# Token high parts from the uncorrected reciprocal root, first transform loads from a second queue, a written order for groups 1 to 7

## The chip, the cores and the metric

The kernel runs on one core of one Trainium2 chip. The metric is the device time of one execution in microseconds (us); lower is better. A time is given as the median of several executions; the profile is of one further execution, with every instruction's start and length. Engines are named as in the profile: PE is TensorE's matmul and PEld its weight load, DVE is VectorE, ACT is ScalarE, POOL is GpSimd, SP is SyncE, which here only issues DMAs.

## What is computed

```python
xn = (x - mean) / sqrt(var + 1e-5)            # x: 2048 tokens x 640
a, b = xn @ dft_hid_re.T, xn @ dft_hid_im.T   # 640 x 640
y = dft_seq_re @ a - dft_seq_im @ b           # 2048 x 2048
h = relu(xn @ W_gate) * (xn @ W_up)           # 640 x 1728
out = x + y + h @ W_down
```

All in float32. The change touches the layernorm `xn` and the first products of the sequence transform with it.

## The kernel before

**Split operands.** Each float32 operand of a matmul is split into a high part (rounded to the matmul's type) and a low part (the rest). A product is three matmuls, high x high, high x low and low x high (`mm3`, lines 129 to 131; `wh`, `wl` are the parts of the weight, `mh`, `ml` those of the moving operand). ScalarE makes a high part by a copy, VectorE the low part by a subtraction (`split`, lines 123 and 124).

**Stages.** First the sequence transform is applied to the normalised tokens, then come gate and up, then the projection. Only the beginning of the first stage is touched. The 2048 tokens form 8 groups (`NG`) of 256: two tiles (`SG`) of 128 partitions each. Groups 0 to 3 have their split tokens in `xs_early`, 4 to 7 in `xs_late`. The transform's output positions form four chunks `c` of 512. The first streams are `B11` (groups 0 to 3) and `B21` (groups 4 to 7), and they run in the order group 0 chunk 0, group 0 chunk 1, group 1 chunk 0, and so on to group 7. Each such pair of group and chunk loads 512 KB of the transform matrix into `raw` (six buffers), splits it into a ring buffer `cb` (three buffers) and runs 18 matmuls into three PSUM banks, two of key `e1` and one of key `v1`. At group 3 the banks' sums are copied out by ScalarE into `sa` (chunk 0) and `sb` (chunk 1); groups 4 to 7 go on adding into the same banks.

**Layernorm of a group.** `ln_load` (198) brings the tokens. `ln_stats` (203, 204) takes two half statistics and an aggregate per tile on VectorE. `ln_root` takes the root (210) on ScalarE, its reciprocal (213) on VectorE, and corrects it by one Newton step of three small VectorE instructions (215 to 217), for which ScalarE prepares the variance with epsilon (211) and the negated mean (212). The corrected `r` stands in `stat`. Then the tokens are centred and scaled, split into high and low parts, and the last 256 columns are kept apart by a DMA from GpSimd (`keep_a21`, 234).

**The order.** Instructions of each engine run in the order in which they are recorded; a scheduler chooses this order from due times, except where `tc.keep_in_program_order` pins an instruction at its place, or `tc.issue_after` holds it behind another. `first_group` pins group 0 by hand, tile by tile. Its token high part waits for the corrected `r` (`ln_scale`, 229 and 230). The first product (`first_products`, 493) has its own order of matmuls, and GpSimd helps with three of the low parts (289). `second_group` handles group 1 with part of its work pinned (products: `second_products`, 465). `layernorm` handles groups 2 to 7, nothing of which is pinned: it scales both tiles in place (246 on VectorE, 247 on ScalarE), copies the high part (120) and subtracts for the low part (251). From group 2 on all products are `product` with `mm3`: one bank after another, 6 matmuls each.

`drive` walks the list `todo` of (load, prepare, run, finish): loads four steps ahead, preparation two steps ahead of the matmuls, and `finish` (the copies out of the banks) one step behind them. All loads are issued by SyncE, in the order x tile 0, chunk 0 half 0, chunk 1 half 0, x tile 1, chunk 1 half 1, chunk 0 half 1, and then tokens and transform blocks in turn.

Of the kernel before, what the change touches and what calls it, by code (L numbers as in the profile page):

```python
# [7 lines left out]
F32 = mybir.dt.float32  # L8
# [4 lines left out]
P = 128  # L13
# [45 lines left out]
def fnet_reglu_kernel(  # L59
# [40 lines left out]
    wparts = dram_p.tile([P, NPAIR, NW], F32, name="wparts")  # L100
    nc.vector.memset(eps_t, EPS)

    root_t = keep.tile([P, 1], F32, name="root_t")
    nc.scalar.activation(root_t, eps_t, AF.Sqrt)

# [85 lines left out]
    def ln_tiles(g):  # L191
        return (ln_place(g),
                small.tile([P, SG, 2, nc.vector.BN_STATS_DIM], F32, name="bs"),
                small.tile([P, SG, 7], F32, name="mv"))

# [10 lines left out]
    def ln_root(g, mv, js, between=()):  # L206
# [19 lines left out]
    def ln_scale(g, xs, j, cs):  # L226
        xc, r = xs[:, j, cs], stat[:, 1, g, j : j + 1]
        h, l = (tokens(g)[:, j * XS + o : j * XS + o + D][:, cs] for o in (0, D))
        yield nc.scalar.activation(h, xc, AF.Copy, scale=r)
        yield nc.vector.scalar_tensor_tensor(l, xc, r, h.bitcast(F32), op0=OP.mult, op1=OP.subtract)  # L230
# [4 lines left out]

    def layernorm(g):
        xs, bs, mv = ln_tiles(g)
        js = slice(0, SG)

        with tc.issue_after(late["ln"]):  # L240
            for i in ln_stats(g, xs, bs, mv, js):
                pass
            for i in ln_root(g, mv, js):
                late["ln"] = i.ins
            nc.vector.tensor_tensor(mv[:, 1, 6:7], stat[:, 0, g, 1:2], stat[:, 1, g, 1:2], op=OP.mult)
            late["norm"] = nc.vector.tensor_scalar(xs[:, 0], xs[:, 0], mv[:, 0, 0:1], stat[:, 1, g, 0:1], op0=OP.subtract, op1=OP.mult).ins
            nc.scalar.activation(xs[:, 1], xs[:, 1], AF.Identity, bias=mv[:, 1, 6:7], scale=stat[:, 1, g, 1:2])
            cs = K14 if g < NH else slice(0, D)
            src = xs[:, :, cs]
            high = copy(xn_block(g, cs, 0), src)  # L250
            low = nc.vector.tensor_tensor(xn_block(g, cs, 1), src, xn_block(g, cs, 0).bitcast(F32), op=OP.subtract)
            if g < NH:
                keep_a21(g)
        if g == 2:
            with tc.issue_after(high.ins), tc.issue_after(low.ins):
                st = stage()[:, :CH].rearrange("p (j d) -> p j d", j=SG)
                for j in range(SG):
                    nc.scalar.activation(st[:, j], ln_place(0)[:, j, K2], AF.Copy, scale=stat[:, 1, 0, j : j + 1])
                keep_a21(0, st)
# [3 lines left out]
    def second_group():  # L263

        xs, bs, mv = late["second"]
        js = slice(0, SG)
        nm, r = (stat[:, i, 1, js] for i in range(2))
        with tc.issue_after(late["ln"]):
            for i in ln_root(1, mv, js):
                tc.keep_in_program_order(i)  # L270
            nmr = mv[:, js, 6]
            late["ln"] = tc.keep_in_program_order(nc.vector.tensor_tensor(nmr, nm, r, op=OP.mult)).ins
            highs = [nc.scalar.activation(xn_block(1, K14, 0)[:, j], xs[:, j, K14], AF.Identity,
                                          bias=mv[:, j, 6:7], scale=stat[:, 1, 1, j : j + 1]) for j in range(SG)]
            for j in range(SG):
                nc.vector.tensor_scalar(xs[:, j], xs[:, j], mv[:, j, 0:1], stat[:, 1, 1, j : j + 1],
                                        op0=OP.subtract, op1=OP.mult)
            low = nc.vector.tensor_tensor(xn_block(1, K14, 1), xs[:, :, K14], xn_block(1, K14, 0).bitcast(F32), op=OP.subtract)
            keep_a21(1)
        late["first"] = [i.ins for i in highs + [low]]  # L280

    def first_group(b):
# [11 lines left out]
        j0, j1 = slice(0, 1), slice(1, 2)  # L294
        d0, d14, rest, every = slice(0, P), slice(P, 3 * P), slice(P, D), slice(0, D)
# [9 lines left out]
        pin(ln_center(0, xs, mv, 0, rest, nc.vector))  # L305
        pin(some(h14, 1))
        pin(high(1, 0))
        pin(h0)
        pin(h14)
        pin(behind(0, token_low(0)))  # L310
        pin(low(nc.gpsimd, 0, 0))
        pin(high(0, 1))
        pin(ln_stats(0, xs, bs, mv, j1))
        pin(low(nc.vector, 1, 0))
        pin(ln_root(0, mv, j1))
        pin(behind(1, stat[:, 1, 0, 1:2]))
        pin(low(nc.gpsimd, 0, 1))
        pin(some(second, 4))
        pin(ln_center(0, xs, mv, 1, every, nc.scalar))
        h0, h14 = ln_scale(0, xs, 1, d0), ln_scale(0, xs, 1, d14)  # L320
        pin(some(h0, 1))
        pin(some(h14, 1))
        pin(high(1, 1))
        pin(h0)
        pin(h14)
        pin(behind(1, token_low(1)))
        pin(low(nc.gpsimd, 1, 1))
        late["ln"] = pin(second)[-1].ins

# [127 lines left out]

    def second_products(b):

        keys = [("e1", 0), ("e1", 1), "v1"]  # L460
        for js, vs in (((0,), (0, 2)), ((1,), (0, 2)), ((0, 1), (1,))):
            for j in js:
                for v in vs:
                    for d, key in zip((0, 1, 4), keys):
                        nc.tensor.matmul(E[0, key], xn_part(SG + j, d)[v == 1], b[:, int(v == 2), j], start=False, stop=False)  # L465

# [17 lines left out]
    def first_products(j, b):  # L484

        keys = [("e1", 0), ("e1", 1), "v1"]
        for v, cs in (((0, (0,)), (1, (0,)), (0, (1,)), (1, (1,)), (2, (0,)), (2, (1,))),
                      ((0, (0,)), (0, (1,)), (2, (0,)), (1, (0,)), (1, (1,)), (2, (1,))))[j]:
            for c in cs:
                for d, key in zip((0, 1, 4), keys):  # L490
                    if j == 0 and v == 0:
                        E[c, key] = bank()
                    nc.tensor.matmul(E[c, key], xn_part(j, d)[v == 1], b[c][0][:, int(v == 2), j],  # L493
                                     start=j == 0 and v == 0, stop=False)
# [18 lines left out]

    start = {}

    def first_stream(c, name, g):
# [5 lines left out]
        norm = {0: 0 if n == 0 else None, 1: n + 1 if n < NG - 1 else None}.get(c)  # L522

        def load():
            if n == 0 and c == 0:
                st = start["raw"] = [raw(), raw()]
                for j in range(SG):
                    ln_load(0, slice(j, j + 1))
                    for k in range(2):
                        i = (k + j) % 2  # L530
                        nc.sync.dma_start(st[i][:, j * CH : (j + 1) * CH], dft[i, 0, 0][:, j * CH : (j + 1) * CH])
                return
            if norm is not None:
                tc.keep_in_program_order(ln_load(norm, slice(0, SG)))
            if n > 0 or c > 1:
                t["s"] = raw()
                nc.sync.dma_start(t["s"], dft[c, 0, n])

        def prepare():
            if norm == 0:  # L540
                start["b"] = [(parts(), st) for st in start["raw"]]
                first_group(start["b"])
                return
            if norm is not None:
                (second_group if norm == 1 else lambda: layernorm(norm))()
            if n > 0 or c > 1:
                t["b"] = b = parts()

                with ExitStack() as order:
                    for i in {(0, 1): [late["ln"]], (1, 1): late.get("first"), (0, 2): [late.get("norm")]}.get((c, n), ()):  # L550
                        order.enter_context(tc.issue_after(i))
                    split(flat(b, 0), flat(b, 1), t["s"])
# [17 lines left out]

        todo.append((load, prepare, run, finish))

# [684 lines left out]
```

## Time and profile before

| | us |
|---|---|
| three timed executions | 1034.75, 1036.84, 1037.27 |
| median | 1036.84 |
| the profiled execution's own time | 1032.92 |
| its span, first to last instruction | 1031.2 |
| TensorE busy in the span | 1022.8 |

How to read the profile: a row of the timeline has the start, the length, the engine, the source line, the operation, what it writes and reads (tile names without their numbers), the shapes, the count of instructions merged into the row, and in brackets how long the engine was idle before it and what released it. A row of the grouped view has a count, the busy time in us, the mean length in ns, and the idle time ahead with its releasers. A row of waits has the engine, tile and line that waited, for whom, the sum in us, how often, and the longest. Matmuls overlap: their length is about 0.39 us, but in a full stream one starts every 0.227 us.

### The profile page before, as it was taken

How to read it: one execution, taken by the hardware profiler on the slowest of the kernel's cores; microseconds unless marked ns; L12 is line 12 of the kernel's file. 1: busy time of each engine (PE TensorE's matmuls, PEld its weight loads, DVE VectorE, ACT ScalarE, POOL GpSimd, SP SyncE). 2: the span in 40 equal slices, each digit the busy share in tenths (PEclk: the TensorE clock that was granted, in tenths of full speed). 3: DMA queues.
4: the chain of work that ended last, by engine and by line, in shares of the span. 5: the costliest groups of instructions: out<-in, count | busy, mean ns of one | idle time of the engine just before them, and what ended most of it. 6: DMA issues, size and time to landing. Idle time of an engine off the chain costs nothing.

```text
span 1031.2 us, 12409 instructions
## 1 busy us (share of the span) xinstructions
PE 1022.8 (99%) x4528; PEld 844.3 (82%) x4528; DVE 800.9 (78%) x1072; ACT 433.3 (42%) x543; POOL 96.6 (9%) x161
## 2 busy tenths in 40 slices
PE   8999999999999999999999999999999999999998
PEld 7888888888888888888888888888888888888886
DVE  7947986978979897688878988886597667886764
ACT  6754443333333543333335443443355423552531
POOL 2000010101211001321110000000000000000000
PEclk9999999999999999999999999999999999999999
DMA  7975744957968864863364665654599647986543
GB/s 301 370 241 163 259 157 143 312 209 254 326 195 298 314 206 153 273 227 133 142 250 143 225 235 215 226 224 156 178 350 296 193 129 225 373 304 222 156 153 122
DMA packets 100156, 233.29 MB, mean 226 GB/s; under 512 B 11392, under 2 KB 50816, under 8 KB 98688
## 3 DMA queue, kind: packets, MB, share of 16 engines
q1 hardware_dynamic: 83088, 163.82, 47.4%
q0 software_dynamic: 17008, 68.69, 18.4%
q8 instruction: 35, 0.57, 0.2%
q14 instruction: 25, 0.20, 0.1%
HBM read 177.41 MB, written 54.02 MB: 224 GB/s over the span
## 4 chain that ended last, share of the span: by engine, by line
PE 96%; DVE 2%; issue 1%; DMA 1%; POOL 0%; SPq 0%; ACT 0%; POOLq 0%; DVEq 0%; ACTq 0%
PE ps L131 31%; PE ps L130 31%; PE ps L129 31%; PE ps L1154 1%; DMA rw<-hd 1%; DVE cb L124 0%; PE ps L493 0%; PE ps L465 0%; POOL cb L289 0%; DVE tk L605 0%; DVE raw L605 0%; DVE st L385 0%; DVE st L378 0%; SPq L1161 0%; DVE st L379 0%
## 5 line engine op out<-in xcount | busy, mean ns | idle before, releaser
L131 PE MATMUL ps<-cb,wt 128*128 128x512 f32 x390 | 151.9, 390 | 0.4 <-DVE wt L124 0.4
L129 PE MATMUL ps<-cb,wt 128*128 128x512 f32 x390 | 151.9, 390 | 0.0
L130 PE MATMUL ps<-cb,wt 128*128 128x512 f32 x390 | 151.8, 389 | 0.0
L124 DVE TENSOR_TENSOR cb<-rw,cb 128x1024 fp32r<-128x1024 f32 x83 | 94.0, 1133 | 68.6 <-ACT cb L123 67.9
L123 ACT ACTIVATE cb<-rw 128x1024 fp32r<-128x1024 f32 x83 | 82.0, 987 | 147.9 <-PE ps L131 127.2
L123 ACT ACTIVATE cb<-raw 128x1024 fp32r<-128x1024 f32 x78 | 82.5, 1059 | 123.5 <-PE ps L131 101.8
L124 DVE TENSOR_TENSOR cb<-raw,cb 128x1024 fp32r<-128x1024 f32 x78 | 95.2, 1221 | 38.9 <-ACT cb L123 38.6
L131 PE MATMUL ps<-xs_early,gw 128*128 128x512 f32 x260 | 101.2, 389 | 0.0
L130 PE MATMUL ps<-xs_early,gw 128*128 128x512 f32 x260 | 101.2, 389 | 0.0
L129 PE MATMUL ps<-xs_early,gw 128*128 128x512 f32 x260 | 101.1, 389 | 0.0
L130 PE MATMUL ps<-cb,xs_late 128*128 128x512 f32 x256 | 99.7, 390 | 0.1
L131 PE MATMUL ps<-cb,xs_late 128*128 128x512 f32 x256 | 99.6, 389 | 0.0
L129 PE MATMUL ps<-cb,xs_late 128*128 128x512 f32 x256 | 99.4, 389 | 0.0
L130 PE MATMUL ps<-cb,xs_early 128*128 128x512 f32 x238 | 92.7, 389 | 0.0
L131 PE MATMUL ps<-cb,xs_early 128*128 128x512 f32 x238 | 92.4, 389 | 0.0
L129 PE MATMUL ps<-cb,xs_early 128*128 128x512 f32 x238 | 92.2, 390 | 0.0
L120 ACT ACTIVATE gw<-z 128x1024 fp32r<-128x1024 f32 (+1 forms) x52 | 57.7, 1110 | 79.3 <-DVE z L776 73.7
L131 PEld LDWEIGHTS ps<-cb,wt 128*128 128x128 f32 x390 | 73.2, 188 | 15.9 <-DVE wt L124 0.7
L130 PEld LDWEIGHTS ps<-cb,wt 128*128 128x128 f32 x390 | 73.2, 188 | 15.7 <-DVE cb L124 0.3
L129 PEld LDWEIGHTS ps<-cb,wt 128*128 128x128 f32 x390 | 73.2, 188 | 15.4 <-ACT wt L123 0.2
L120 ACT ACTIVATE u<-ps 128x512 f32<-128x512 f32 x52 | 31.1, 598 | 96.4 <-PE ps L131 96.4
L786 DVE TENSOR_TENSOR gw<-z,gw 128x1024 fp32r<-128x1024 f32 (+1 forms) x52 | 64.7, 1285 | 2.2 <-ACT gw L120 2.2
(195 smaller groups left out, 1924.7 us busy)
## 6 DMA issues: line engine op xcount, KB each, us to landing
raw<-in_dft SPq DMA_DIRECT2D x94, 512.0 KB, 5.3
wt<-wparts SPq DMA_DIRECT2D x66, 256.0 KB, 3.2
z<-in_wgu SPq DMA_DIRECT2D x26, 640.0 KB, 4.0
hd<-ob POOLq DMA_DIRECT2D x26, 512.0 KB, 3.5
rw<-hd SPq DMA_DIRECT2D x24, 512.0 KB, 6.3
wparts<-pw POOLq DMA_DIRECT2D x11, 1024.0 KB, 4.1
tk<-in_dft SPq DMA_DIRECT2D x16, 512.0 KB, 7.4
rw<-pq SPq DMA_DIRECT2D x16, 512.0 KB, 7.6
```

What stands on the lines that cost most here:

```text
L120: return nc.scalar.activation(o, i, AF.Copy)
L123: nc.scalar.activation(hi, src, AF.Copy)
L124: return nc.vector.tensor_tensor(lo, src, hi.bitcast(F32), op=OP.subtract)
L129: nc.tensor.matmul(ps, wh, mh, start=first, stop=False, skip_group_check=more)
L130: nc.tensor.matmul(ps, wh, ml, start=False, stop=False, skip_group_check=more)
L131: nc.tensor.matmul(ps, wl, mh, start=False, stop=last, skip_group_check=more)
L786: tt(self.w[:, 1, cs], self.z[:, cs], self.w[:, 0, cs].bitcast(F32), op=OP.subtract)
L1154: nc.tensor.matmul(B[key], wr[:, v, es], hr[:, cs], start=False, stop=v == 1, skip_group_check=not new)
```

## The change

1. **Root.** A new `ln_root_fast` replaces `ln_root` in all groups. The token high part is scaled by `r0`, the plain reciprocal of the root (`mv` column 4), instead of the corrected `r`. The low part is still `x * r - high` with the corrected `r`, so high and low together are the same value. The correction comes after the high parts on VectorE. A constant -epsilon/2 (`half_t`) lets ScalarE prepare `-0.5 * var - epsilon/2` for it.
2. **First loads.** The first halves of chunk 0 and chunk 1 (256 KB each) are issued by ScalarE, ahead of its activation table load, instead of SyncE. SyncE issues the two token tiles first, then the two second halves. Later loads of tokens come one step earlier, right behind the chunk 0 block of the group before.
3. **Group 0.** The pinned order changes: the first transform split stands ahead of the first root, only the first 384 columns are centred (both tiles on VectorE), and the roots of the second tile stand ahead of its transform splits. The 256 columns left uncentred are centred when they are kept, by one more ScalarE step per tile.
4. **Groups 1 to 7.** `second_group` and `layernorm` pin every instruction on VectorE and ScalarE, the transform splits of both chunks included. The high part of the tokens is made straight from the raw tokens, tile by tile (scale `r0`, bias `-mean * r0`). The statistics of the next group stand between: one tile ahead of the low part of the tokens, one behind the second chunk's low part.
5. **Products.** Chunk 0 of every group from 1 on uses `early_products`: high tokens first, low tokens last, and the three banks in turn within each set. Chunk 1 keeps `product`. The first products of group 0 are reordered likewise. `finish` runs directly behind the matmuls of its step.

The core of the diff:

```diff
+    def ln_root_fast(g, mv, js):
+        mean, v, ve, sd, r0, t = (mv[:, js, i] for i in range(6))
+        nm, r = (stat[:, i, g, js] for i in range(2))
+        one = nc.vector.tensor_scalar if v.shape[1] == 1 else None
+        yield nc.scalar.activation(sd, v, AF.Sqrt, bias=eps_t)
+        yield nc.vector.reciprocal(r0, sd)
+        yield nc.scalar.activation(ve, v, AF.Identity, bias=half_t, scale=-0.5)
+        yield nc.scalar.activation(nm, mean, AF.Copy, scale=-1.0)
+        if one:
+            yield one(t, r0, ve, r0, op0=OP.mult, op1=OP.mult)
+        else:
+            yield nc.vector.tensor_tensor(t, r0, ve, op=OP.mult)
+            yield nc.vector.tensor_tensor(t, t, r0, op=OP.mult)
+        yield nc.vector.scalar_tensor_tensor(r, t, 1.5, r0, op0=OP.add, op1=OP.mult)
...
-        yield nc.scalar.activation(h, xc, AF.Copy, scale=r)
+        yield nc.scalar.activation(h, xc, AF.Copy, scale=mv[:, j, 4:5])
...
+    def layernorm(g, split_0, split_1, split_last=None):
+        pin = tc.keep_in_program_order
+        high_0, low_0 = split_0
+        xs, bs, mv = late["next"]
+        js = slice(0, SG)
+        cs = K14 if g < NH else slice(0, D)
+        root = ln_root_fast(g, mv, js)
+        for i in split_last or ():
+            pin(i())
+        if g == 2:
+            pin(high_0())
+        for i in range(2):
+            pin(next(root))
+        pin(nc.vector.scalar_tensor_tensor(mv[:, js, 6], mv[:, js, 0], -1.0, mv[:, js, 4], op0=OP.mult, op1=OP.mult))
+        pin(next(root))
+        if g > 2:
+            pin(high_0())
+        for j in range(SG):
+            pin(nc.scalar.activation(xn_block(g, cs, 0)[:, j], xs[:, j, cs], AF.Identity,
+                                     bias=mv[:, j, 6:7], scale=mv[:, j, 4:5]))
+        for i in root:
+            pin(i)
+        pin(nc.vector.scalar_tensor_tensor(mv[:, 1, 7:8], mv[:, 1, 0:1], -1.0, stat[:, 1, g, 1:2], op0=OP.mult, op1=OP.mult))
+        pin(nc.scalar.activation(xs[:, 1], xs[:, 1], AF.Identity, bias=mv[:, 1, 7:8], scale=stat[:, 1, g, 1:2]))
+        pin(low_0())
+        pin(nc.vector.tensor_scalar(xs[:, 0], xs[:, 0], mv[:, 0, 0:1], stat[:, 1, g, 0:1], op0=OP.subtract, op1=OP.mult))
+        next_stats(g + 1, 1)
+        pin(nc.vector.tensor_tensor(xn_block(g, cs, 1), xs[:, :, cs], xn_block(g, cs, 0).bitcast(F32), op=OP.subtract))
+        if g < NH:
+            keep_a21(g)
+        for i in split_1 if g != NH else ():
+            pin(i())
+        next_stats(g + 1, 1)
...
         pin(ln_stats(0, xs, bs, mv, j0))
-        pin(ln_center(0, xs, mv, 0, d0, nc.vector))
-        pin(ln_root(0, mv, j0))
         pin(high(0, 0))
-        h0, h14 = ln_scale(0, xs, 0, d0), ln_scale(0, xs, 0, d14)
+        root = ln_root_fast(0, mv, j0)
+        pin(some(root, 1))
+        pin(ln_center(0, xs, mv, 0, K14, nc.vector))
+        pin(some(root, 2))
+        h0, h14 = ln_scale(0, xs, mv, 0, d0), ln_scale(0, xs, mv, 0, d14)
...
-    def second_products(b):
+    def early_products(n, b):
         keys = [("e1", 0), ("e1", 1), "v1"]
         for js, vs in (((0,), (0, 2)), ((1,), (0, 2)), ((0, 1), (1,))):
             for j in js:
                 for v in vs:
                     for d, key in zip((0, 1, 4), keys):
-                        nc.tensor.matmul(E[0, key], xn_part(SG + j, d)[v == 1], b[:, int(v == 2), j], start=False, stop=False)
+                        nc.tensor.matmul(E[0, key], xn_part(n * SG + j, d)[v == 1], b[:, int(v == 2), j], start=False,
+                                         stop=n % NH == NH - 1 and (j, v) == (SG - 1, 1), skip_group_check=n >= NH)
...
-                        nc.sync.dma_start(st[i][:, j * CH : (j + 1) * CH], dft[i, 0, 0][:, j * CH : (j + 1) * CH])
-                return
+                        (nc.sync if j else nc.scalar).dma_start(st[i][:, j * CH : (j + 1) * CH], dft[i, 0, 0][:, j * CH : (j + 1) * CH])
+                nc.scalar.activation(root_t, eps_t, AF.Sqrt)
...
-            if n == 1 and c == 0:
-                second_products(t["b"])
+            if c == 0:
+                early_products(n, t["b"])
                 return
...
-        todo.append((load, prepare, run, finish))
+        todo.append((load, prepare, lambda: (run(), finish()), idle))
```

More of the change, by code (lines that the diff above doesn't have):

```diff
@@ L265, in second_group @@
+    def second_group(split_0, split_1):
+        pin = tc.keep_in_program_order
+        (high_0, low_0), (high_1, low_1) = split_0, split_1
         xs, bs, mv = late["second"]
         js = slice(0, SG)
[L267 to L279, printed above, removed]
@@ L280, in second_group @@
-        late["first"] = [i.ins for i in highs + [low]]
+        root = ln_root_fast(1, mv, js)
+        for i in range(2):
+            pin(next(root))
+        pin(nc.vector.scalar_tensor_tensor(mv[:, js, 6], mv[:, js, 0], -1.0, mv[:, js, 4], op0=OP.mult, op1=OP.mult))
+        pin(next(root))
+        pin(high_0())
+        for j in range(SG):
+            pin(nc.scalar.activation(xn_block(1, K14, 0)[:, j], xs[:, j, K14], AF.Identity,
+                                     bias=mv[:, j, 6:7], scale=mv[:, j, 4:5]))
@@ L282, in first_group @@
+        for j in range(SG):
+            pin(nc.scalar.activation(st[:, j], ln_place(0)[:, j, K2], AF.Identity, bias=stat[:, 0, 0, j : j + 1]))
+            pin(nc.scalar.activation(st[:, j], st[:, j], AF.Copy, scale=stat[:, 1, 0, j : j + 1]))
+        keep_a21(0, st)
+        pin(low_1())
+        next_stats(2, 2)
     def first_group(b):
@@ L294, in first_group @@
         j0, j1 = slice(0, 1), slice(1, 2)
[L295 removed]
+        d0, d14 = slice(0, P), slice(P, 3 * P)
         late["second"] = ln_tiles(1)
@@ L512, in sums_b @@
         return sums.tile([P, 4, CH], F32, name="sb")
-    start = {}
+    start, streams = {}, {}
     def first_stream(c, name, g):
```

109 lines of the change are left out of this document (59 added, 50 removed).

## The prediction

> **What bounds the kernel now.** I read first the busy shares, then the span cut at the points where TensorE starts something new (columns: length, busy time and instruction count of PE, PEld, DVE, ACT, POOL, then clock, DMA share, GB/s), then what TensorE waited for.
>
> ```profile
> span 1031.2 us, 12409 instructions
> PE 1022.8 (99%) x4528; PEld 844.3 (82%) x4528; DVE 800.9 (78%) x1072; ACT 433.3 (42%) x543; POOL 96.6 (9%) x161
> ```
> ```profile
> 0.00:6.58 6.58, 4.16 (x49) 3.99 (x49) 2.60 (x12) 3.03 (x8) 0.20 (x4) 1.00 0.71 212
> 6.58:16.43 9.85, 9.04 (x37) 6.80 (x38) 8.30 (x25) 6.91 (x16) 4.28 (x6) 1.00 1.02 408
> 16.43:41.20 24.77, 24.77 (x110) 20.11 (x108) 23.72 (x55) 17.66 (x33) 3.19 (x5) 1.00 0.85 320
> 100.00:1000.00 900.00, 899.47 (x3962) 743.07 (x3961) 710.30 (x901) 369.25 (x443) 86.85 (x143) 1.00 0.66 224
> 1026.60:1031.20 4.60, 0.00 (x0) 0.00 (x0) 0.69 (x1) 0.00 (x0) 0.00 (x0) 1.00 0.31 114
> ```
> ```profile
> PE ps L493 <- ACT xs_early L229: 1.9, 2, 1.4
> PE ps L493 <- POOL cb L289: 0.3, 1, 0.3
> ```
>
> TensorE is the bound: 899.47 us for 3962 matmuls is 0.227 us each, without gaps and at the full clock. The change takes no matmul away, so only time in which TensorE is not paced by itself can be won. Behind some 110 us every engine has the same instructions in the same order in both kernels, and the last 4.6 us are untouched. What is left is the beginning: the 36 matmuls of group 0 take 9.85 us where 36 x 0.227 = 8.2 would do, so 1.6 are lost there; the 108 of groups 1 to 3 take 24.77 instead of 24.5, so 0.25 are lost; and the first real matmul starts at 6.58. A hard ceiling follows: 1.6 + 0.25 + whatever the start itself gains.
>
> **Part 1: the start (6.58).** The chain to the first matmul:
>
> ```profile
> 0.75 0.38 SPq L198 DMA_DIRECT2D r<-in_x  x1
> ...
> 1.18 0.90 SPq L531 DMA_DIRECT2D raw<-in_dft  x2
> ...
> 3.77 0.89 DVE L203 BATCH_NORM_STATS2 bs<-r 128x6 f32<-128x320 f32 x2 [2.79 <-DMA r<-in_x]
> ...
> 4.93 0.29 ACT L210 ACTIVATE mv<-mv,eps_t 128x1 f32<-128x1 f32 x1 [2.69 <-DVE mv L204]
> ...
> 5.26 0.16 DVE L213 RECIPROCAL mv<-mv 128x1 f32<-128x1 f32 x1
> ...
> 6.12 0.91 ACT L229 ACTIVATE xs_early<-r,stat 128x128 fp32r<-128x128 f32 x2
> ...
> 6.58 4.57 PE L493 MATMUL ps<-cb,xs_early 128*128 128x512 f32 x18 [1.39 <-ACT xs_early L229]
> ```
>
> Scaling by the reciprocal itself takes the three correction steps (5.26 + 0.20 to 6.12) off the chain: 0.86 become 0.20, a saving of 0.66. Against it stands the load. The first half of the tokens was alone in the DMA engines; now ScalarE issues the first transform half (256 KB) at the same moment.
>
> ```profile
> 2.00:3.74 1.74, 1.74 (x19) 1.74 (x18) 0.00 (x0) 0.23 (x2) 0.00 (x0) 1.00 0.82 288
> ```
>
> At 288 GB/s (the rate while that load ran) 0.26 MB are 0.9 us, at the later 408 0.64: if the two streams alternate, the statistics start 0.6 to 0.9 later; if the engines, busy to 0.82, have room for both, 0 later. I take 0.7, being nearer to the shared end since 0.82 leaves little room. The start then moves by -0.66 + 0.7: 6.6 again; the ends are 5.9 and 6.8. [...]
>
> ```profile
> 0.74 1.28 ACT L104 ACT_TABLE_LOAD   x1 [0.74 <-PEq L1250]
> ```
>
> The activation table load, now behind two issues (0.90 for two, above), is done near 3.2 and hidden: ScalarE's first data comes after 3.7.
>
> **Part 2: group 0, second tile.**
>
> ```profile
> 7.47 0.88 DVE L203 BATCH_NORM_STATS2 bs<-r 128x6 f32<-128x320 f32 x2
> ...
> 9.23 0.63 ACT L288 ACTIVATE cb<-raw 128x512 fp32r<-128x512 f32 x1 [1.68 <-DMA raw<-in_dft]
> 9.77 0.28 ACT L210 ACTIVATE mv<-mv,eps_t 128x1 f32<-128x1 f32 x1
> ...
> 11.22 0.80 ACT L229 ACTIVATE xs_early<-r,stat 128x128 fp32r<-128x128 f32 x2
> ...
> 12.45 4.13 PE L493 MATMUL ps<-cb,xs_early 128*128 128x512 f32 x17 [0.27 <-POOL cb L289]
> ```
>
> ```profile
> L204 DVE BATCH_NORM_AGGREGATE mv<-bs 128x2 f32<-128x12 f32 x16 | 3.3, 204 | 0.2
> ```
>
> In before the root (9.77) stood behind a split that waited for its load until 9.23, though the statistics were done near 7.47 + 0.88 + 0.2. Now the root comes first: 8.45, reciprocal 8.8, token high parts 9.0 to 9.8, then the split 9.7 to 10.3. TensorE needs them at 6.6 + 18 x 0.227 + 0.1 = 10.8. Both stalls go; group 0 would end at 14.9. The other split that changes places, the first one, now ahead of the first root, takes the same 0.63 and costs at most 0.1: it starts when its data lands, about a microsecond ahead of the root.
>
> **Part 3: group 1 is late next.**
>
> ```profile
> 10.85 0.89 DVE L203 BATCH_NORM_STATS2 bs<-r 128x6 f32<-128x320 f32 x2
> ...
> 13.66 0.30 ACT L210 ACTIVATE mv<-mv,eps_t 128x2 f32<-128x2 f32 x1 [0.17 <-DVE mv L204]
> ...
> 15.28 1.31 ACT L273 ACTIVATE xs_early<-r,mv,stat 128x384 fp32r<-128x384 f32 x2 [1.04 <-DVE mv L272]
> ...
> 16.43 4.24 PE L465 MATMUL ps<-cb,xs_early 128*128 128x512 f32 x18
> ```
> ```profile
> L123 ACT ACTIVATE cb<-raw 128x1024 fp32r<-128x1024 f32 x4 | 4.2, 1058 | 1.6 <-PE ps L131 1.6
> ```
>
> Its load lands near 10.85 (the DMA share is 1.02 up to there, so no earlier). Two pairs of statistics and two aggregates are 2 x 0.88 + 0.4 = 2.2: the root at 13.05, the reciprocal at 13.4. ScalarE's list then has the transform split (1.05) and the high parts (0.65 each): the first is ready at 15.1, the second at 15.7, when TensorE has reached only the fourth pair. **TensorE starts group 1 at 15.2 instead of 16.43: 1.2 won.** Since this hangs on the load of group 1, the start may lie anywhere from 5.9 to 6.8 without changing it. The first 12 of the group's 18 matmuls now need no low part of the tokens, which is ready at 17.7 and needed at 15.2 + 2.7 = 17.9.
>
> **Part 4: the written order of groups 2 to 7.**
>
> ```profile
> L124 DVE TENSOR_TENSOR cb<-raw,cb 128x1024 fp32r<-128x1024 f32 x13 | 15.8, 1213 | 0.1
> L203 DVE BATCH_NORM_STATS2 bs<-r 128x6 f32<-128x320 f32 x32 | 14.4, 475 | 2.8 <-DMA r<-in_x 2.8
> L251 DVE TENSOR_TENSOR xs_late<-r,xs_late 128x1280 fp32r<-128x1280 f32 x4 | 6.0, 1488 | 0.6 <-ACT xs_late L120 0.6
> L246 DVE TENSOR_SCALAR r<-r,mv,stat 128x640 f32<-128x640 f32 x6 | 3.6, 608 | 0.0
> L213 DVE RECIPROCAL mv<-mv 128x2 f32<-128x2 f32 x7 | 1.1, 164 | 0.7 <-ACT mv L210 0.7
> L251 DVE TENSOR_TENSOR xs_early<-r,xs_early 128x768 fp32r<-128x768 f32 x2 | 1.9, 946 | 0.0
> ```
> ```profile
> L247 ACT ACTIVATE r<-r,mv,stat 128x640 f32<-128x640 f32 x3 | 2.8, 925 | 1.9 <-DVE mv L245 1.9
> L120 ACT ACTIVATE sa<-ps 128x512 f32<-128x512 f32 x3 | 1.8, 593 | 0.3 <-PE ps L131 0.3
> ```
>
> An instruction's successor starts some 0.08 before its end (the pair at 7.47). VectorE's list per group: six small ones 1.1, two lows 2 x 1.13, one scaling 0.52, four statistics and two aggregates 2.1, the low part of the tokens 0.86 (1.40 from group 4 on), and one exposed trip to ScalarE for the root, 0.37: 7.2, then 7.75. TensorE takes 36 x 0.227 = 8.2 per group, so VectorE keeps ahead and the order costs nothing by itself. ScalarE's additions (high parts tile by tile, 0.6 a group; two more steps for the kept columns, 0.8 once) fit beside its 17.66 busy of 24.77.
>
> But the new product order of stream c = 0 writes its three banks in turn, so they are complete only at the end of group 3's stream, and group 4 writes all three within its first three matmuls. They have to be copied out between. VectorE's list, followed from 13.4: group 1 ends its lows at 18.85, group 2's reciprocal is at 21.35, group 3's at 28.5, group 4's at 35.8. ScalarE then runs without a break from the root at 35.5: split to 36.85, two high parts of 640 to 38.5, first copy 39.1, the scaling of the second tile (0.83) to 39.95, copies to 40.55 and 41.05. TensorE, at 15.2 + 24.5 + 0.1, is there at 39.8: its third matmul waits until 41.1, 0.85 late.
>
> ```profile
> 40.20 0.58 ACT L120 ACTIVATE sa<-ps 128x512 f32<-128x512 f32 x1
> ...
> 41.20 0.39 PE L129 MATMUL ps<-cb,xs_late 128*128 128x512 f32 x1
> ```
>
> In before the last of those copies ended at 40.78, group 4 started at 41.20 and its third matmul stood at 41.65. **The sum: 41.1 against 41.65, 0.5 us won, 0.7 given back.** Behind it VectorE gains 0.4 a group on TensorE and nothing more stalls. Bounds: VectorE's chain of 25 us by 3% either way is 0.7, so the gain lies between about -0.3 and the 1.2 of part 3.
>
> The profiled execution is 1032.92 us, span and 1.7 around it; by the sum it becomes 1032.4. The three timed runs have their median at 1036.84 (1034.75 to 1037.27), 3.9 higher; I take the same 0.5 off it: **1036.3**.
>
> **The rivals.**
> - *The copies are in time*, since VectorE's list runs quicker or group 1 lands earlier: 1.2 to 2 us won, 1035.2. For it: VectorE has hardly a gap in before either, and ScalarE has gaps. Against: the copies stand behind a chain without slack.
> - *The new order does not do what it says*: the start is slowed by sharing and group 0 keeps a stall because the second stream's first half, now in the queue beside the tokens, lands later than TensorE's fourth matmul wants it. Gain 0 to -0.5 us: 1036.9.
> - *Slower: VectorE's list becomes the bound from group 4 to 7.* The list blocks in order: a low waits for ScalarE's split, which waits for a free ring buffer, and the next group's statistics stand behind it. Slack is 8.2 - 7.75 = 0.45 a group; with two more exposed trips of 0.6 each a group takes 8.95, and four groups cost 3.0, less what was won: 1039.4. It decides from 0.45 of added waiting a group. For it: VectorE is 23.72 busy of 24.77 between 16.43 and 41.20. Against: the ring lets a split run a whole group ahead.
>
> **How the numbers follow.** Forecast 0.58, copies in time 0.22, no gain 0.11, slower 0.09. A measurement of this kernel tells about 0.3% (3.1 us) from no change. The ceiling of part 1 and 2, 1.6 + 0.25 + 0.66 = 2.5 us, lies under that, so faster by more comes only from scatter of the runs on top of the second case: 0.07. Slower by more needs most of the last rival: 0.08. The rest, 0.85, is the same. The range takes the ceiling (1034.3) and the run's scatter of about 1.2 on both sides of the first three cases: 1033.8 to 1038.2.
>
> **What would show it.** In the changed profile: the first real matmul near 6.6 with its statistics near 4.4 (sharing) or near 5.9 with 3.8 (none); no idle of TensorE within the first 36 matmuls; group 1 near 15.2; the matmuls of group 4 waiting for ScalarE's copies near 40 to 41; nothing between 42 and 100. Wrong would be a stall in groups 5 to 7 put down to VectorE, or a first stage slower than 9.85.

## The result, and the profile after

| | before | after |
|---|---|---|
| median, us | 1035.80 (1032.55 to 1037.27, 4 executions) | 1049.76 (1048.65 to 1050.32, 4 executions) |
| ratio | | 1.0151, 95% interval 1.0137 to 1.0166 |
| profiled execution, its span | 1032.92, 1031.2 | 1049.69, 1047.9 |

The changed kernel is 1.5% slower, about 14 us; the forecast was no change. The first two lines of the page of after already say something odd: the same number of matmuls (4528), TensorE busy for 99% of the span as before, and yet 17 us more of it.

```profile
span 1047.9 us, 12409 instructions
PE 1039.9 (99%) x4528; PEld 845.4 (81%) x4528; DVE 803.8 (77%) x1077; ACT 434.7 (41%) x550; POOL 96.5 (9%) x160
```

The waits of TensorE in after. There is one real one, ahead of the first product; no list of VectorE or ScalarE holds it up later:

```profile
PE ps L548 <- ACT xs_early L246: 2.0, 1, 2.0
PE ps L112 <- DVE warm L108: 1.1, 1, 1.1
PE ps L132 <- DVE wt L125: 0.4, 1, 0.4
```

So the time went into busy TensorE. The span of after, cut as that of before was:

```profile
6.58:16.43 9.85, 9.18 (x33) 7.19 (x34) 8.54 (x28) 6.51 (x17) 4.12 (x5) 0.83 1.03 417
16.43:41.20 24.77, 24.77 (x108) 19.90 (x107) 22.41 (x55) 17.20 (x32) 3.08 (x4) 1.00 0.78 281
100.00:1000.00 900.00, 899.64 (x3902) 731.53 (x3900) 702.92 (x893) 365.47 (x439) 85.25 (x140) 1.00 0.65 222
```

Between 100 and 1000 us TensorE starts 3902 matmuls instead of 3962, at a granted clock of 1.00 (full speed, the third column from the right) and without waiting. Three windows, one in each stage (first stage, gate and up, projection), show where. Before:

```profile
60.00:120.00 60.00, 60.00 (x266) 49.71 (x265) 38.03 (x47) 27.22 (x36) 2.13 (x4) 1.00 0.63 210
430.00:730.00 300.00, 300.00 (x1325) 248.34 (x1324) 240.90 (x383) 119.73 (x164) 31.36 (x54) 1.00 0.56 197
780.00:1000.00 220.00, 220.00 (x971) 181.90 (x970) 157.19 (x166) 91.13 (x102) 8.70 (x16) 1.00 0.69 229
```

After:

```profile
60.00:120.00 60.00, 60.00 (x258) 48.17 (x258) 38.47 (x51) 29.66 (x41) 2.13 (x4) 1.00 0.60 189
430.00:730.00 300.00, 300.00 (x1300) 243.74 (x1299) 243.78 (x389) 120.51 (x164) 36.43 (x60) 1.00 0.57 198
780.00:1000.00 220.00, 220.00 (x972) 181.98 (x970) 161.57 (x171) 97.46 (x111) 7.08 (x13) 1.00 0.72 239
```

258 matmuls instead of 266 in the first stage, 1300 instead of 1325 in gate and up, the same 972 and 971 in the projection. The instructions behind 110 us are the same ones in the same order, so something other than the order sets the pace.

**What differs is where the tiles lie.** The new constant `half_t` is a tile of 128 x 1 float32. In the built program it takes 32 bytes of each partition, ahead of everything that the pools put on the left side of SBUF. So all left tiles (`cb`, `raw`, `r1`, the first weight set `gw`, `wt`, `sets_b`) lie 32 bytes further, and the right ones (`xs_early`, `xs_late`, the second `gw`) where they were. In before every operand of nearly every matmul starts at a multiple of 512 bytes; two padding tiles called `edge` see to that (constants `LEDGE`, `EDGE`). Taking the two operands of each matmul from the built program, and the distance between the starts of neighbouring matmuls from the trace, gives for after, in the largest groups (distances under 330 ns alone, so without waits and without the half clock):

| moving operand and weights | matmuls | ns from one start to the next, mean |
|---|---|---|
| `cb` (left) with `xs_late` (right) | 767 | 233.3 |
| `cb` (left) with `xs_early` (right) | 760 | 233.3 |
| `xs_early` (right) with first `gw` (left) | 390 | 233.5 |
| `xs_early` (right) with second `gw` (right) | 390 | 229.2 |
| `cb` (left) with `wt` (left): the projection | 1167 | 226.9 |

In before every such row is 226.7 to 227.0. Operands on different sides of SBUF, 32 bytes apart from agreeing, take 233.3 to 233.5 ns, 6.6 more; 2298 matmuls of the program are of that kind (768, 768 and 390 of the first three rows, and three smaller groups of 168, 144 and 60). 2298 x 6.6 ns is 15.2 us. **Theory A**: the pace depends on how the starts of the two operands stand to each other. **Rivals**: B, the half clock of the beginning leaves a slow pace behind; C, the new order of products and lists sets the pace; D, the place of a tile itself counts, not the difference.

The beginning has changes of its own. From the timeline of after (start, length, engine):

```profile
0.74 0.89 ACTq L588 DMA_DIRECT2D raw<-in_dft  x2
0.75 0.86 SPq L199 DMA_DIRECT2D r<-in_x  x2
...
5.11 0.89 DVE L204 BATCH_NORM_STATS2 bs<-r 128x6 f32<-128x320 f32 x2 [4.11 <-DMA r<-in_x]
...
6.27 0.29 ACT L225 ACTIVATE mv<-mv,eps_t 128x1 f32<-128x1 f32 x1 [0.35 <-DVE mv L205]
...
6.80 0.80 ACT L246 ACTIVATE xs_early<-r,mv 128x128 fp32r<-128x128 f32 x2
...
7.25 10.26 PE L548 MATMUL ps<-cb,xs_early 128*128 128x512 f32 x36 [1.96 <-ACT xs_early L246]
...
13.92 0.30 ACT L225 ACTIVATE mv<-mv,eps_t 128x2 f32<-128x2 f32 x1 [1.94 <-DVE mv L205]
...
15.26 1.29 ACT L314 ACTIVATE xs_early<-r,mv 128x384 fp32r<-128x384 f32 x2
...
17.35 2.96 PE L519 MATMUL ps<-cb,xs_early 128*128 128x512 f32 x12
```

The statistics start at 5.11 (before 3.77), the first product at 7.25 (6.58), group 1 at 17.35 (16.43). The 36 matmuls of group 0 now run in one row, without a wait, but take 10.1 us; the clock column of the first window above says 0.83. After 1.96 us of idling, eight matmuls start 0.43 to 0.51 us apart.

### The profile page after: what moved, and what is told of

It is laid out like the page before. It is cut to its first block, busy times and chain, and to the rows that moved or that the text cites. A ratio compares the mean times of both kernels' runs of the same rounds, so it can differ in the third digit from the quotient of the medians.

```text
span 1047.9 us, 12409 instructions
## 1 busy us (share of the span) xinstructions
PE 1039.9 (99%) x4528; PEld 845.4 (81%) x4528; DVE 803.8 (77%) x1077; ACT 434.7 (41%) x550; POOL 96.5 (9%) x160
## 4 chain that ended last, share of the span: by engine, by line
PE 98%; DMA 1%; DVE 0%; issue 0%; ACT 0%; SPq 0%; ACTq 0%
PE ps L130 31%; PE ps L132 31%; PE ps L131 31%; PE ps L519 3%; PE ps L548 1%; PE ps L1226 1%; DMA rw<-hd 1%; DMA r<-in_x 0%; SPq L1233 0%; ACT cb L124 0%; DVE wt L125 0%; DVE bs L204 0%; DVE y L1236 0%; DVE r L239 0%; ACT xs_early L246 0%
## 5 line engine op out<-in xcount | busy, mean ns | idle before, releaser
L124 ACT ACTIVATE cb<-raw 128x1024 fp32r<-128x1024 f32 x64 | 67.9, 1060 | 121.7 <-PE ps L132 96.2
L125 DVE TENSOR_TENSOR cb<-raw,cb 128x1024 fp32r<-128x1024 f32 x64 | 78.1, 1221 | 40.3 <-ACT cb L124 40.2
L131 PE MATMUL ps<-xs_early,gw 128*128 128x512 f32 x260 | 102.5, 394 | 0.0
L130 PE MATMUL ps<-xs_early,gw 128*128 128x512 f32 x260 | 102.4, 394 | 0.0
L132 PE MATMUL ps<-xs_early,gw 128*128 128x512 f32 x260 | 102.0, 392 | 0.0
L131 PE MATMUL ps<-cb,xs_late 128*128 128x512 f32 x232 | 91.8, 396 | 0.0
L132 PE MATMUL ps<-cb,xs_late 128*128 128x512 f32 x232 | 91.6, 395 | 0.0
L130 PE MATMUL ps<-cb,xs_late 128*128 128x512 f32 x232 | 91.5, 395 | 0.0
L131 PE MATMUL ps<-cb,xs_early 128*128 128x512 f32 x226 | 89.3, 395 | 0.0
L132 PE MATMUL ps<-cb,xs_early 128*128 128x512 f32 x226 | 89.3, 395 | 0.0
L130 PE MATMUL ps<-cb,xs_early 128*128 128x512 f32 x226 | 89.0, 395 | 0.0
L130 PEld LDWEIGHTS ps<-cb,wt 128*128 128x128 f32 x390 | 73.2, 188 | 15.2
L121 ACT ACTIVATE u<-ps 128x512 f32<-128x512 f32 x52 | 31.1, 598 | 104.5 <-PE ps L132 104.5
```

Source lines behind the costliest of these rows:

```text
L121: return nc.scalar.activation(o, i, AF.Copy)
L124: nc.scalar.activation(hi, src, AF.Copy)
L125: return nc.vector.tensor_tensor(lo, src, hi.bitcast(F32), op=OP.subtract)
L130: nc.tensor.matmul(ps, wh, mh, start=first, stop=False, skip_group_check=more)
L131: nc.tensor.matmul(ps, wh, ml, start=False, stop=False, skip_group_check=more)
L132: nc.tensor.matmul(ps, wl, mh, start=False, stop=last, skip_group_check=more)
```

## The experiments

All times are beside executions of the kernel before on the same chip, with a median of 1033.0, 1033.5 and 1033.27 us in the three sets. A ratio is reckoned from the single executions and can differ a little from that of the two medians.

### Undo the 32 bytes (e_fix)

```diff
-LEDGE, EDGE = 448, 480
+LEDGE, EDGE = 416, 480
```

> The changed kernel with one number changed: the padding tile `edge` of the pool `keep` shrinks from 448 to 416 bytes, so that every tile on the left side of SBUF stands again where it stood before the new constant `half_t` took 32 bytes ahead of it. No instruction changes. Theory A (matmuls whose moving operand and weights do not start at the same place modulo 64 bytes start every 0.2333 us instead of every 0.2267 us; 2298 of the 4528 are such): 2298 x 6.6 ns = 15.2 us go, time 1034.6 us, first stage at 0.227 us a matmul (431 -> 440 matmuls between 100 and 200 us). Rival B (the half clock near 7 to 10 us leaves a slow pace behind) and rival C (the new order of the products and of the pinned lists sets the pace): nothing moves, 1049.8 us, 431 matmuls between 100 and 200 us.

Measured: 1034.31 us (1032.12 to 1037.06), ratio 1.0008 (0.9997 to 1.002). Not one instruction differs from after, and the 15 us are gone; the three windows hold 267, 1325 and 971 matmuls:

```profile
60.00:120.00 60.00, 60.00 (x267) 49.68 (x266) 41.61 (x55) 30.17 (x42) 2.13 (x4) 1.00 0.61 202
430.00:730.00 300.00, 300.00 (x1325) 248.47 (x1324) 240.75 (x385) 119.24 (x163) 32.98 (x55) 1.00 0.56 197
780.00:1000.00 220.00, 220.00 (x971) 181.99 (x970) 157.71 (x168) 90.19 (x103) 8.70 (x16) 1.00 0.68 230
```

C falls. B does not fall by this run alone, since its profiled execution had no half clock at the start either (1.00 from 7.24 to 16.00).

### Put the 32 bytes into the kernel before (e_before_left32)

```diff
-LEDGE, EDGE = 448, 480
+LEDGE, EDGE = 480, 480
```

> The kernel before with one number changed: the padding tile on the left grows from 448 to 480 bytes, so that the left tiles are 32 bytes off as in the changed kernel. No instruction changes. Theory A: the slow pace appears in the kernel before, 0.2333 us a matmul in the first stage, 0.2267 us again in the projection, time 1035.8 + 15.2 = 1051 us. Rivals B and C: no change, 1035.8 us.

Measured: 1048.77 us (1047.77 to 1050.68), ratio 1.0150 (1.0132 to 1.0168), which is the whole loss of the change. B falls here: one of the four executions had a mean granted clock of 1.000, so no 3.4 us at half the clock, and took 1047.77 us all the same; and e_fix_banks below has the half clock at the start and then starts a matmul every 0.227 us (18 from 21.35 to 25.43). The windows of this kernel, whose instructions are those of before:

```profile
60.00:120.00 60.00, 60.00 (x259) 48.25 (x258) 36.11 (x43) 26.35 (x36) 2.13 (x4) 1.00 0.58 197
430.00:730.00 300.00, 300.00 (x1300) 243.89 (x1299) 243.46 (x389) 120.53 (x164) 35.74 (x59) 1.00 0.56 197
780.00:1000.00 220.00, 220.00 (x971) 182.10 (x970) 161.59 (x171) 96.93 (x110) 7.08 (x13) 1.00 0.72 238
```

### Shift both sides (e_both32)

```diff
-LEDGE, EDGE = 448, 480
+LEDGE, EDGE = 448, 448
```

> The changed kernel with the padding tile on the right side of SBUF cut from 480 to 448 bytes: the left tiles stay 32 bytes off, and the right tiles (the split tokens and one set of weights) move 32 bytes too. No instruction changes. Theory A (only the difference between the two operands counts): all 4528 matmuls agree again, 1034.6 us, 0.2267 us throughout. Rival D (what counts is the place of a tile itself, not the difference): all matmuls are at the slow pace, the projection too, 1049.8 + 2230 x 6.6 ns = 1064.5 us. Rivals B and C: 1049.8 us.

Measured: 1033.11 us (1032.77 to 1036.90), ratio 1.0004 (0.9994 to 1.0015). Every tile is 32 bytes off a multiple of 512, and the pace is that of before:

```profile
60.00:120.00 60.00, 60.00 (x266) 49.67 (x266) 41.32 (x54) 30.17 (x43) 2.13 (x4) 1.00 0.62 207
430.00:730.00 300.00, 300.00 (x1325) 248.35 (x1324) 240.83 (x383) 119.30 (x163) 31.69 (x53) 1.00 0.56 198
780.00:1000.00 220.00, 220.00 (x971) 181.94 (x970) 157.37 (x166) 91.50 (x103) 8.70 (x16) 1.00 0.69 230
```

D falls: it is the difference between the two operands that counts. The tiles that the other engines read and write moved too in these runs, but the projection, whose operands both lie on the left, keeps its 971 or 972 matmuls in every one of them; so moving those tiles does not slow TensorE by itself.

### By how much may they differ? (e_before_left64, 128, 256, 512)

All four are the kernel before with another `LEDGE`: 512, 576, 704, 960.

> The kernel before with the left padding tile at 512 bytes: left tiles 64 bytes off. Theory A with 64 bytes as the modulus: no change, 1035.8 us, 0.2267 us a matmul throughout. A variant of theory A with a modulus of 128 bytes or more: the slow pace as with 32 bytes off, 1051 us.

> The kernel before with the left padding tile at 576 bytes instead of 448: left tiles 128 bytes off. With 64 bytes off the first stage ran at 0.2289 us a matmul and gate and up at 0.2311, so 64 is not the modulus of theory A. If it is 128: no change, 0.2267 us throughout, time as before (1033.0 us). If it is 256 or more: a slow pace again, at least the 1042.7 us of 64 bytes off.

> The kernel before with the left padding tile at 704 bytes instead of 448: left tiles 256 bytes off. With 128 bytes off the time was 1048.2 us. If the modulus of theory A is 256: no change, about 1033.5 us, 0.2267 us throughout. If it is 512 or more: a slow pace again where the operands disagree, 1042 to 1049 us.

> The kernel before with the left padding tile at 960 bytes: left tiles 512 bytes off, so that all operands start again at multiples of 512 bytes. Theory A with a modulus of 512 (or a divisor of it): no change, about 1033.5 us, 0.2267 us throughout. If the pace depended on the distance itself, or on a modulus of 1024 or more: slow, 1042 to 1049 us.

| left tiles off by | matmuls in 60:120, 430:730, 780:1000 | median, us | ratio (interval) |
|---|---|---|---|
| 0 (before) | 266, 1325, 971 | 1033.0 to 1033.5 | 1 |
| 32 | 259, 1300, 971 | 1048.77 | 1.0150 (1.0132 to 1.0168) |
| 64 | 264, 1300, 971 | 1042.73 | 1.0097 (1.0070 to 1.0124) |
| 128 | 259, 1303, 971 | 1048.21 | 1.0134 (1.0116 to 1.0152) |
| 256 | 266, 1326, 971 | 1033.37 | 0.9995 (0.9985 to 1.0006) |
| 512 | 267, 1325, 971 | 1033.71 | 1.0006 (0.9993 to 1.0020) |

My first guess of 64 bytes for the modulus was wrong, and so was 128. Of the distances tried, those that are multiples of 256 cost nothing and the others cost 1 to 1.5%. With 64 bytes the first stage loses less (0.2289 us a matmul) than gate and up (0.2311). Why is not settled. The profiled execution of 64 bytes (1047.21 us) is the slowest of its four and has a half clock of its own between 300 and 400 us (a mean of 0.98 there); the windows in the table lie clear of it.

### The first loads alone (e_before_queue)

```diff
-    nc.scalar.activation(root_t, eps_t, AF.Sqrt)
...
-                        nc.sync.dma_start(st[i][:, j * CH : (j + 1) * CH], dft[i, 0, 0][:, j * CH : (j + 1) * CH])
+                        (nc.sync if j else nc.scalar).dma_start(st[i][:, j * CH : (j + 1) * CH], dft[i, 0, 0][:, j * CH : (j + 1) * CH])
+                nc.scalar.activation(root_t, eps_t, AF.Sqrt)
```

> The kernel before with one part of the change alone: the first halves of chunk 0 and chunk 1 issued by ScalarE ahead of its table load. No new tile, no other order. Theory A: the pace stays 0.2267 us; the statistics start near 5.1 instead of 3.77, as in the changed kernel, so the first matmul near 7.9 (before's 6.58 plus 1.34); the rest of the group waits less on its loads, and the time is 0.3 to 1.3 us over that of before. Rival (the second queue itself slows the matmuls, for instance through the loads that ScalarE's table load now follows): a pace of 0.233 us, 1048 us.

Measured: 1039.87 us (1038.35 to 1041.77), ratio 1.0056 (1.0035 to 1.0076). The pace is 0.227 us (22 matmuls from 33.81 to 38.80), so the queue doesn't set it. The start came as expected (first matmul at 7.84), but the loss of 6.4 us is far more than the 0.3 to 1.3 that I gave. The waits of TensorE in this kernel:

```profile
PE ps L128 <- ACT xs_early L119: 2.4, 1, 2.4
PE ps L492 <- ACT xs_early L228: 2.3, 1, 2.3
...
PE ps L128 <- ACT wt L122: 0.9, 1, 0.9
```

Behind each of the three the clock fell to half: its mean is 0.83 from 7.84 to 17.75 and 0.93 from 17.75 to 42.42, 3.4 us at half the clock each, and the 0.995 of the whole span leaves as much for the third. The first one is new: in the list of before ScalarE took the root of group 2 and then split a transform block; here the scheduler put the split ahead. It stood idle for 2.90 us, with the root and all that hangs on it behind. The row names no releaser; by the times it waited for a ring buffer, as the 18 matmuls on group 1's chunk 0 end at 21.99.

```profile
22.07 1.06 ACT L122 ACTIVATE cb<-raw 128x1024 fp32r<-128x1024 f32 x1 [2.90 <-issue]
23.04 0.28 ACT L209 ACTIVATE mv<-mv,eps_t 128x2 f32<-128x2 f32 x1
```

So this run isn't the price of the queue alone: the unpinned list moved with it. The half clock is not the whole loss either: of the four executions, one had a mean granted clock of 1.000 and still took 1038.35 us. In the third wait, near 753 us, the split of `wt` stands behind one that waited until 751.74 for its load (`rw` from `hd`); why this load came late is open.

### The copies out of the banks (e_fix_banks)

With the pace right, e_fix shows the stall that the prediction forecast for group 4. From its timeline:

```profile
39.45 0.60 ACT L121 ACTIVATE sa<-ps 128x512 f32<-128x512 f32 x1
39.94 0.91 ACT L279 ACTIVATE r<-r,mv,stat 128x640 f32<-128x640 f32 x1
40.67 0.39 PE L519 MATMUL ps<-cb,xs_late 128*128 128x512 f32 x1
40.76 1.07 ACT L121 ACTIVATE sa<-ps 128x512 f32<-128x512 f32 x2
...
41.39 4.41 PE L519 MATMUL ps<-cb,xs_late 128*128 128x512 f32 x17 [0.33 <-ACT sa L121]
```

TensorE is there at 40.67, writes the first bank and waits for the copies of the other two, which stand behind the scaling at 39.94. The 18 matmuls take until 45.64, 4.97 us instead of 4.08. The edit, for group 4 only and on top of the padding of e_fix:

```diff
+        if n == NH:
+            for d, key in zip((0, 1, 4), keys):
+                for j, v in ((0, 0), (0, 2), (1, 0), (1, 2)):
+                    nc.tensor.matmul(E[0, key], xn_part(n * SG + j, d)[0], b[:, int(v == 2), j], start=False, stop=False,
+                                     skip_group_check=True)
-        for js, vs in (((0,), (0, 2)), ((1,), (0, 2)), ((0, 1), (1,))):
+        for js, vs in (((0,), (0, 2)), ((1,), (0, 2)), ((0, 1), (1,)))[2 if n == NH else 0:]:
```

> The changed kernel with the left padding tile at 416 bytes, and in group 4 the products of chunk 0 take the high tokens bank by bank (4 matmuls a bank) instead of the three banks in turn; the low tokens stay last. The profiled execution with the padding alone lost 0.89 us there: matmul 192 at 40.67, matmul 210 at 45.64, 4.97 us for 18 matmuls that take 4.08 at pace. Theory (the copies of group 3's banks into `sa` hold TensorE up): the second and third bank are needed at 41.6 and 42.5, the copies end at 41.3 and 41.8, so the stall goes: matmul 210 at 44.75, 0.9 us less than with the padding alone, 1033.4 us beside 1034.3. Rival (the wait is of ScalarE's whole list and only moves): no change.

Measured: 1032.52 us (1031.61 to 1033.97), ratio 0.9985 (0.9975 to 0.9996). The stall is gone, but this profiled execution doesn't show it cleanly: half the clock at the start had made TensorE come a microsecond later (41.75), when two copies were done and the last ended at 42.00. The next kernel shows it. The median is 1.8 us under that of e_fix, twice the 0.9 that I gave; the two runs are of different sets, and what makes the rest is not shown.

### Bank by bank, and the first loads on SyncE again (e_fix_banks_sync)

```diff
-                        (nc.sync if j else nc.scalar).dma_start(st[i][:, j * CH : (j + 1) * CH], dft[i, 0, 0][:, j * CH : (j + 1) * CH])
-                nc.scalar.activation(root_t, eps_t, AF.Sqrt)
+                        nc.sync.dma_start(st[i][:, j * CH : (j + 1) * CH], dft[i, 0, 0][:, j * CH : (j + 1) * CH])
```

The table load goes back to its place at the top, by the activation on `root_t`.

> The kernel of e_fix_banks with all first loads issued by SyncE in the order of before, ScalarE's table load first as before. Theory (the four shared loads cost the beginning 1.3 us, and group 1's load limits its start): statistics at 3.8, first matmul near 5.9, group 1 at 15.2 instead of 16.0, so 0.8 us less than e_fix_banks and 1.3 less than before: 1031.7 us beside 1033.0 of before. Rival (the loads behind the first ones then come too late, as the changed order needs the second chunk earlier): a stall in group 0 and no gain, 1033 us.

Measured: **1031.30 us** (1030.47 to 1032.67), ratio 0.9974 (0.9963 to 0.9986): faster than both kernels. From its timeline:

```profile
3.75 0.89 DVE L205 BATCH_NORM_STATS2 bs<-r 128x6 f32<-128x320 f32 x2 [2.75 <-DMA r<-in_x]
...
6.12 8.54 PE L554 MATMUL ps<-cb,xs_early 128*128 128x512 f32 x36
...
12.68 0.30 ACT L226 ACTIVATE mv<-mv,eps_t 128x2 f32<-128x2 f32 x1 [1.94 <-DVE mv L206]
...
14.76 3.51 PE L525 MATMUL ps<-cb,xs_early 128*128 128x512 f32 x14
```

First product at 6.12, group 1 at 14.76 where before had 16.43. Group 4 comes at 39.44, earlier than in e_fix, and its 18 matmuls take 4.10 us, though the last copy ends only at 40.60: the bank order removes the stall. At matmul 1400 of the trace this kernel is 1.67 us ahead of before (313.88 against 315.56).

### No idling ahead of the first product (e_fix_banks_warm)

```diff
-WARM = 48
+WARM = 78
```

> The kernel of e_fix_banks with 78 instead of 48 matmuls on the tile of zeros ahead of the first product, so that TensorE is not idle before the first real matmul. In the profiled execution of e_fix_banks the idle of 2.13 us was followed by 3.15 us at half the clock, which cost 1.5 us. Theory (an idle stretch of about 2 us brings the half clock): no matmul at 0.42 us, matmul 84 at 16.0 instead of 17.27, time 1031 to 1032 us beside the 1032.5 of e_fix_banks. Rival (the half clock comes from the load on the engines at that time, whatever TensorE did before): it stays, 1032.5 us, or a little more where the added matmuls hold up the first real one.

The first products in the profiled execution of e_fix_banks, and of this kernel:

```profile
7.42 10.01 PE L553 MATMUL ps<-cb,xs_early 128*128 128x512 f32 x36 [2.13 <-ACT xs_early L246]
```
```profile
7.19 8.71 PE L553 MATMUL ps<-cb,xs_early 128*128 128x512 f32 x36 [0.29 <-ACT xs_early L246]
```

With the idle stretch (0.29 us are left of 2.13) the half clock went (1.00 from 7.25 to 17.40), and the 36 matmuls take 8.7 instead of 10.0 us. The time did not follow: 1032.42 us (1031.47 to 1037.05), ratio 0.9988 (0.9974 to 1.0002), no better than e_fix_banks. That the half clock came with the idling and went with it in these two profiled executions is shown; that it costs the median anything is not. Of the twelve executions of e_fix_banks eight had a mean granted clock of 1.000 anyway, with a median of 1032.2 us; the four others took 1032.69 to 1033.15.

## Why the prediction was wrong

**The step that failed** is the first: "899.47 us for 3962 matmuls is 0.227 us each, without gaps and at the full clock. The change takes no matmul away, so only time in which TensorE is not paced by itself can be won." The pace was taken for a constant of TensorE. In these runs it goes with the layout of SBUF: 226.7 to 227.0 ns in before, 233.3 to 233.5 in after for operands 32 bytes off. The change adds a tile of 32 bytes a partition, and my list of parts has no line for it: `half_t` was costed at nothing without a word. The same blind spot made the ceiling of 2.5 us one-sided: it bounded what could be won, and nothing bounded what could be lost where "TensorE is paced by itself". Undone, the ratio falls from 1.0151 to 1.0008, which is 14.8 us of 1033 (e_fix); put into before, the shift costs 15.8, 1048.77 less 1033.0 (e_before_left32); 2298 x 6.6 ns makes 15.2.

These runs show what the distance of the two operands costs: with the same instructions in the same order, 60 us of the first stage hold 266 matmuls in before and 259 in e_before_left32, 300 us of gate and up 1325 and 1300. What in the hardware makes the difference is not shown.

The other steps can be read from after and, without the shift, from e_fix and e_fix_banks_sync:

- *Part 1, the shorter chain.* Right: from the statistics to the first product 2.14 us (5.11 to 7.25) where before took 2.81 (3.77 to 6.58), 0.67 saved; I had 0.66.
- *Part 1, the shared loads.* The kind was right, the size wrong. I took 0.7 with an end at 0.9; it is 1.34 (3.77 to 5.11). By my estimate not two but four loads shared the time: both token halves and both transform halves had been issued by 1.63 us, and from there to 5.11 the two queues of after moved 0.61 and 0.36 MB, in 61.8 and 31.1% of the engines' time. Nor was the first token half alone in before: 288 GB/s over 1.74 us are 0.50 MB, and it has 0.33. With SyncE alone the statistics start at 3.75 (e_fix_banks_sync). The first product came at 7.25, outside the 5.9 to 6.8 that I gave.
- *The idling.* Not foreseen: in the profiled execution of after TensorE is idle for 1.96 us ahead of the first product instead of 1.39, and the clock then fell to half for 3.4 us (0.50 from 7.41 to 10.82). The later start makes only part of it. In e_fix the first product comes at 7.24 too, but the 48 matmuls on zeros ahead of it took longer, the idling was 1.33 us, and group 0 took 8.76 us instead of 10.1. The matmuls on zeros of after, and below them those of e_fix:

```profile
1.06 4.23 PE L112 MATMUL ps<-warm 128*128 128x128 bf16 x48 [1.06 <-DVE warm L108]
1.06 4.85 PE L112 MATMUL ps<-warm 128*128 128x128 bf16 x48 [1.06 <-DVE warm L108]
```

  They start 0.107 us apart at first and under 0.06 later; the slow pace lasts for some 27 of them in after and 39 in e_fix. With the same instructions the half clock came in one of these two profiled executions and not in the other.
- *Part 2.* Right: both stalls of group 0 are gone, one row of 36 matmuls in each kernel with the new order. It takes 8.64 us up to group 1 in e_fix_banks_sync and 8.76 in e_fix, where 8.2 was forecast; in both, the last 0.3 of it is group 1 waiting for its first high part.
- *Part 3.* The mechanism was right, with the wrong limit in after: group 1's first high part is ready near 15.9, but TensorE comes only at 17.35. In e_fix it starts at 16.00, with the first loads on SyncE at 14.76; forecast 15.2. What failed is "the start may lie anywhere from 5.9 to 6.8 without changing it": e_fix_banks_sync has its first product 1.12 us earlier than e_fix (6.12 and 7.24) and group 1's root 1.24 earlier (12.68 and 13.92). In both, group 1's statistics follow group 0's low part on VectorE without idling (10.52 and 11.77), so VectorE's list sets them and not the load. The row at 10.85 of before, read as the landing, shows no idling ahead of it either.
- *Part 4.* VectorE's list is no bound, as forecast. The stall of group 4 was forecast at 0.85 us and measured at 0.89 in e_fix; in after it is hidden, since TensorE comes at 42.55, after the last copy (41.82).
- *The rivals.* None had the layout. What the change was about does come out near the forecast, 1.0008 without the shift where 1036.3 of 1036.84 is 0.9995, but in part by luck: group 1 comes 0.8 us later than forecast, and at the end of group 4's first 18 matmuls e_fix is 0.36 us behind before (45.64 and 45.28), not 0.5 ahead.

## What to carry to other kernels

Where a kernel has padding tiles or odd sizes in its pools, a new tile ahead of them is an edit of the layout: compare where every matmul operand lies in both builds before costing anything else, and compare the number of matmuls in equal windows of a stage before looking for a wait. A busy share of 99% doesn't mean that the pace is the best one (before and after both have it, at 1035.80 and 1049.76 us), and "the bound engine does the same work" is no bound on its time. A stall that hides behind a slower pace can come back when the pace is mended (0.89 us at group 4 in e_fix, none in after), so forecasts of both are worth keeping.

## What was not expected of the hardware

- Matmuls (128x512, float32) whose two operands lie 32 bytes off from agreeing start every 233.3 to 233.5 ns in after; in before, where they agree, it is every 226.7 to 227.0. Shifts of 64 and 128 bytes cost too (264 and 259 matmuls in 60 us of the first stage where before has 266, 1300 and 1303 in 300 us of gate and up where it has 1325), shifts of 256 and 512 do not (266 and 267, 1326 and 1325). Matmuls that agree but stand in a mixed stream lose too (229.2 ns in the row of `xs_early` with the second `gw`).
- The granted clock fell to half after TensorE idled for 1.96 us (after: 0.50 from 7.41 to 10.82), 2.13 (e_fix_banks: a mean of 0.998 over the span), 2.31 and 2.43 (e_before_queue: 0.83 from 7.84 to 17.75, 0.93 from 17.75 to 42.42), and not after 1.27 (e_both32), 1.33 (e_fix) or 1.39 (before), with 1.00 in the windows behind each. Of pairs of idle stretches close together, 1.3 and 0.5 us brought it in e_before_left64 (0.98 from 300 to 400) and 0.9 and 0.4 in e_before_queue (the third there, 0.995 over the span), and 1.4 and 0.5 didn't in e_fix_banks_sync (1.000 over the span). So the idle time alone doesn't tell these cases apart; what does is not shown.
- Some profiled executions have a wait near 355 us and others don't, though the instructions there are the same: between matmuls 1500 and 1600 e_fix lost 1.2 us and e_fix_banks_sync 2.4 us that e_fix_banks did not lose. No edit here touches that stretch; how often it happens was not measured.
